# Attention with a gated spectral branch: spectral part added in the output PSUM tile, gate folded into its operand, one order of value matmuls for each kind of group, a table of keys, partial output tiles

## The chip, the cores and the metric

The kernel runs on one core of a Trainium2 chip. The metric is the device time of that core in microseconds (us), the median of several executions. Each execution also has a mean granted clock of TensorE (1.0 is full speed) and a state: "slow" when the run is over 1.5% above the fastest of the same kernel. Ratios are computed from the mean time of one kernel's fast runs over the mean time of the other's fast runs of the same rounds on the same chip, so they are not quite the ratio of the medians that are quoted. The kernel before took 421.3 us in the first measurement.

## The reference, cut to what matters

```python
def reference(A_x, A_wqkv, A_wo, B_x, B_w_r, B_w_i, gate_w):   # x: 2048 tokens x 448
    x = A_x
    g = sigmoid((x * gate_w).sum(-1, keepdims=True))           # one gate for each token
    a = full_softmax_attention(x, A_wqkv, A_wo)                # 16 heads of 28
    b = irfft2(rfft2(x) * (B_w_r + 1j * B_w_i)).astype(bf16)   # spectral mix over tokens and features
    return g * a + (1 - g) * b
```

## The kernel before

The kernel is built by a list scheduler in Python: each operation has an engine, a duration, dependences and a key (when it is due), and a simulated run fixes the order in which each engine's instructions are emitted. Each engine has its own stream of instructions in that order, with semaphores between the engines.

Attention goes over 16 groups (4 head groups x 4 chunks of 512 queries), each with 16 key tiles. TensorE makes the scores; ScalarE takes their exponentials, 3 or 2 units of 128x512 at a time, into a ring of 30 units. For some key tiles VectorE does the exponential instead: it evicts the score tile (y), and makes four shifted tiles from the integer bits (pd). TensorE multiplies ring and pd by the values (vw for the ring, vd for VectorE's tiles). The list ND says how many key tiles of each group VectorE takes, 37 in all:

```python
    ND = [0, 2, 2, 2, 2, 3, 2, 3, 2, 2, 3, 2, 3, 3, 3, 3]
```

The weights vd of VectorE's tiles are made on GpSimd, four times for each head group, each piece over three key tiles:

```python
            for f in range(4):
                def fp(f=f):
                    self.pin(nc.gpsimd.tensor_scalar(out=self.vd[:, f, :, :, 0:DH + 1], in0=self.vf[:],
                                                     scalar1=PHGAIN[f], scalar2=None, op0=ALU.mult))
```

In the background, between these, runs the spectral branch: two stages of Fourier matmuls in which a tile is evicted to one of three buffers Y and copied by DMA into a re-ordered buffer U. At its end, each output tile of 128 tokens is evicted (zt), multiplied by a last basis matrix, scaled by the complement of the gate on the way out of PSUM, and kept in SBUF (bm) until the attention part of the tile is there:

```python
            def fz(it=it, zt=zt):
                self.pin(nc.vector.tensor_copy(out=zt[0:FN].rearrange("p a b -> p (a b)"), in_=self.bgi(it)[0:FN, :]))
            # [cut: four matmuls zt x Binv into a second PSUM tile it2]
            def fb_(g=g, it2=it2):
                self.pin(nc.vector.tensor_scalar(out=self.bm[:, g, 0:D], in0=self.bgi(it2)[:, 0:D],
                                                 scalar1=self.og[:, g:g + 1], scalar2=None, op0=ALU.mult))
            # [cut]
            # output tile t, after four matmuls by wo:
            self.pin(nc.vector.scalar_tensor_tensor(out=fin[:], in0=self.bgi(it)[:, 0:D], scalar=self.gs[:, t:t + 1],
                                                    in1=self.bm[:, t, 0:D], op0=ALU.mult, op1=ALU.add))
```

All value matmuls of a group are issued in one fixed order, whether their operand comes from the ring or from VectorE: each depends on the one before (`deps = [prev_pv]`).

## Time and profile before

| | kernel before |
|---|---|
| median | 421.31 us (420.91 to 426.13) |
| span of the profiled run | 420.0 us, granted clock 0.996 |
| first exponential starts | 10.99 us |
| last exponential ends | 409.84 us |
| ScalarE busy | 403.2 us (96%) |
| VectorE busy | 349.9 us (83%) |

From the page of the kernel before: the span, the busy time of each engine, then the busy tenths of ScalarE and the granted clock in 40 slices of the span, then the share of the engines in the chain that ended last.

```profile
span 420.0 us, 12309 instructions
PE 390.9 (93%) x5207; PEld 150.9 (36%) x5207; DVE 349.9 (83%) x660; ACT 403.2 (96%) x370; POOL 30.3 (7%) x63
...
ACT  4999999999999999999999999999999999999991
...
PEclk9999999999999999999999999999899999999999
...
ACT 62%; PE 19%; issue 15%; DVE 1%; DMA 1%; ACTq 0%; DVEq 0%
```

And its costliest groups: busy time and mean length of one, then the idle time of the engine just before them and what ended most of it.

```profile
L1141 ACT ACTIVATE ring<-psA 128x1536 bf16<-128x1536 f32 x176 | 286.9, 1630 | 1.6 <-PE bg L544 0.7
L1141 ACT ACTIVATE ring<-psB 128x1024 bf16<-128x1024 f32 x175 | 212.2, 1213 | 0.0
L1099 DVE TENSOR_SCALAR y<-bg 128x512 uint16<-128x512 f32 x148 | 99.7, 684 | 14.6 <-PE bg L544 11.5
L1109 DVE TENSOR_SCALAR pd<-y 128x2048 uint16<-128x2048 uint16 x148 | 99.2, 686 | 0.6
```

ScalarE is busy from the second slice to the last but one, and its 351 exponentials are preceded by 1.6 us of idle time in all. The stream of exponentials is the bound. In these names psA and psB are the score tiles of three and of two units, bg the two PSUM banks for the background work, and pvb the bank of the value matmuls. Read in the timeline of ScalarE, the starts of two exponentials that follow each other without a stop are taken as 1.343 us apart after one of three units and 0.917 us after one of two, so 2.26 us for a pair (most lie between 1.330 and 1.347 us, and between 0.903 and 0.922 us). In the rest of this document "the stream lost" means: the time from the first to the last start of an exponential, less the sum of these two numbers over the exponentials between. The kernel before lost 2.6 us in that sense.

### The profile page before, as it was taken

What the parts mean: (1) busy time and instruction counts of PE and PEld (TensorE: products, weight loads), DVE (VectorE), ACT (ScalarE), POOL (GpSimd) and SP (SyncE); (2) the same over time, 40 slices, a digit from 0 to 9 for tenths busy, and PEclk for the clock granted to TensorE, in tenths of its full rate; (3) what the DMA queues carried; (4) which work ended last, traced back from release to release, by engine and by line L of the source; (5) the groups of instructions that cost most, each with busy time, mean ns of one, the idle gap of its engine ahead of it and who ended that gap; (6) DMA issues with size and microseconds to landing.
All of it is one profiled execution on the core that took longest, in us unless ns stands there. A gap on an engine that the chain in (4) does not pass through costs nothing.

```text
span 420.0 us, 12309 instructions
## 1 busy us (share of the span) xinstructions
PE 390.9 (93%) x5207; PEld 150.9 (36%) x5207; DVE 349.9 (83%) x660; ACT 403.2 (96%) x370; POOL 30.3 (7%) x63
## 2 busy tenths in 40 slices
PE   7899999999999989898998999899999999999996
PEld 5444333333443233233433334334343233323334
DVE  5555878878787999999989998986878999798964
ACT  4999999999999999999999999999999999999991
POOL 4302200000004000000040000000021000000000
PEclk9999999999999999999999999999899999999999
DMA  8500010001412211100110112211001110100011
GB/s 221 138 2 4 6 37 2 3 2 48 119 47 69 70 48 43 23 25 22 25 43 14 34 47 83 63 34 30 1 4 54 27 27 2 45 3 23 26 35 55
DMA packets 25915, 16.85 MB, mean 40 GB/s; under 512 B 10456, under 2 KB 24580, under 8 KB 25860
## 3 DMA queue, kind: packets, MB, share of 16 engines
q1 hardware_dynamic: 25092, 15.82, 14.3%
q8 instruction: 40, 0.66, 0.7%
q10 hardware_dynamic: 768, 0.25, 0.3%
q14 instruction: 15, 0.12, 0.1%
HBM read 10.19 MB, written 1.84 MB: 29 GB/s over the span
## 4 chain that ended last, share of the span: by engine, by line
ACT 62%; PE 19%; issue 15%; DVE 1%; DMA 1%; ACTq 0%; DVEq 0%
ACT ring L1141 61%; PE bg L544 8%; PE psA L544 4%; PE pvb L544 3%; PE psB L544 3%; DMA U<-in_A_wqkv_dram 1%; ACT w L947 0%; DVE k L888 0%; DVE q L888 0%; DVE q L735 0%; DVE k L904 0%; DVE xT L842 0%; ACT fin L1338 0%; ACT sq L718 0%; ACT q L719 0%
## 5 line engine op out<-in xcount | busy, mean ns | idle before, releaser
L1141 ACT ACTIVATE ring<-psA 128x1536 bf16<-128x1536 f32 x176 | 286.9, 1630 | 1.6 <-PE bg L544 0.7
L1141 ACT ACTIVATE ring<-psB 128x1024 bf16<-128x1024 f32 x175 | 212.2, 1213 | 0.0
L1099 DVE TENSOR_SCALAR y<-bg 128x512 uint16<-128x512 f32 x148 | 99.7, 684 | 14.6 <-PE bg L544 11.5
L544 PEld LDWEIGHTS <-k 32*128 32x128 bf16 (+1 forms) x1088 | 50.1, 91 | 140.5 <-issue 131.7
L1109 DVE TENSOR_SCALAR pd<-y 128x2048 uint16<-128x2048 uint16 x148 | 99.2, 686 | 0.6
L544 PE MATMUL psA<-q,k 32*128 32x512 bf16 x526 | 70.0, 383 | 18.1 <-ACT ring L1141 13.6
L544 PE MATMUL pvb<-ring,vw 128*32 128x512 bf16 x876 | 80.9, 387 | 0.0
L544 PE MATMUL psB<-q,k 32*128 32x512 bf16 x350 | 69.0, 382 | 2.5 <-ACT ring L1141 2.0
L544 PE MATMUL pvb<-pd,vd 128*32 128x512 bf16 x592 | 58.7, 386 | 0.0
L544 PE MATMUL bg<-q,k 32*128 32x512 bf16 x148 | 54.7, 384 | 0.3 <-DVE fin L1360 0.2
L544 PEld LDWEIGHTS <-vw 128*32 128x32 bf16 x876 | 21.6, 96 | 19.2 <-issue 15.4
L544 PEld LDWEIGHTS <-xT 128*128 128x128 bf16 (+3 forms) x512 | 19.2, 96 | 17.1 <-issue 14.5
L1434 DVE CAST Y<-bg 128x450 bf16<-128x450 f32 x32 | 19.6, 622 | 4.4 <-PE bg L544 3.1
L1008 POOL TENSOR_SCALAR vd<-vf 128x348 bf16<-128x348 f32 x16 | 17.6, 1101 | 59.9 <-DVE vf L997 43.1
L544 PE MATMUL bg<-X,R 128*32 128x225 bf16 (+1 forms) x384 | 20.7, 295 | 0.6 <-DVE y L1099 0.2
L544 PEld LDWEIGHTS <-vd 128*32 128x32 bf16 x592 | 15.4, 95 | 15.5 <-issue 13.6
L544 PE MATMUL bg<-xT,wpq 128*32 128x512 bf16 (+1 forms) x240 | 19.1, 383 | 0.0
L544 PE MATMUL bg<-xT,wpk 128*32 128x512 bf16 (+2 forms) x244 | 18.8, 382 | 0.0
L544 PE MATMUL bg<-Bd,xT 128*32 128x450 bf16 (+1 forms) x256 | 17.9, 358 | 0.3
L544 PE MATMUL bg<-Bd,ZT 113*32 113x448 bf16 x256 | 17.6, 357 | 0.3 <-DVE y L1099 0.2
L952 POOL CAST vw<-w 128x16 bf16<-128x16 f32 (+1 forms) x7 | 2.4, 349 | 192.1 <-ACT w L947 192.1
L1404 DVE CAST X<-bg 128x450 bf16<-128x450 f32 x16 | 10.0, 624 | 7.4 <-PE bg L544 7.4
(119 smaller groups left out, 340.1 us busy)
## 6 DMA issues: line engine op xcount, KB each, us to landing
U<-Y SPq DMA_DIRECT2D x32, 112.5 KB
CR<-cRB SPq DMA_DIRECT2D x8, 256.0 KB
xtok<-in_A_x_dram SPq DMA_DIRECT2D x4, 448.0 KB
out_dram<-fin SPq DMA_DIRECT2D x14, 112.0 KB
CR<-cCS SPq DMA_DIRECT2D x8, 192.0 KB
Wg<-in_B_w_r_dram SPq DMA_DIRECT2D x8, 112.5 KB
Wg<-in_B_w_i_dram SPq DMA_DIRECT2D x8, 112.5 KB
U<-in_A_wqkv_dram SPq DMA_DIRECT2D x2, 252.0 KB
```

Of the source, the lines that this page charges most:

```text
L544: self.pin(self.nc.tensor.matmul(out, lhsT=lhsT, rhs=rhs, start=start, stop=stop, **kw))
L952: self.pin(nc.gpsimd.tensor_copy(out=free_dims(self.vw[g][:], [[128, nb], [32, 4]], kt0 * 128 + DH), in_=self.w[g][:, kt0:kt0 + nb, :]))
L1008: self.pin(nc.gpsimd.tensor_scalar(out=self.vd[:, f, :, :, 0:DH + 1], in0=self.vf[:], scalar1=PHGAIN[f], scalar2=None, op0=ALU.mult))
L1099: self.pin(nc.vector.tensor_scalar(out=ys[:, s, :], in0=self.bgi(it), scalar1=127 * UNITS, scalar2=0.0, op0=ALU.add, op1=ALU.max))
L1109: self.pin(nc.vector.tensor_scalar(out=fl(pds).bitcast(U16), in0=fl(ys), scalar1=float(PHASE[f]), scalar2=0.25, op0=ALU.add, op1=ALU.mult))
L1141: self.pin(nc.scalar.activation(out=self.ring[:, u0:u0 + len(st), :], in_=slot[:, 0:len(st), :], func=ACT.Exp, scale=LN2 / UNITS))
L1404: self.pin(nc.vector.tensor_copy(out=self.X1[:, t, :], in_=self.bgi(it)[:, 0:F2]))
L1434: self.pin(nc.vector.tensor_copy(out=y[:], in_=self.bgi(it)[:, 0:F2]))
```

## The change

The intent is to give ScalarE less to do. Six more key tiles go to VectorE, and VectorE gets the room for it from the spectral branch: its result is no longer evicted on its own, but accumulated by TensorE into the same PSUM tile as the attention part of the output. As the eviction multiplies that tile by g, the spectral operand has to be multiplied by (1 - g)/g beforehand. That is a factor for each token, needed along the free dimension, the same in all partitions; so the gate, which lies one token to a partition, is written to DRAM and read back as rows. The buffer that receives the rows is the space of the transposed input xT, free by then: the profile calls the read "xT<-escr". Besides: the value matmuls keep an order only within their kind (ring, VectorE); six of the last eight output tiles are collected early in SBUF ("partial"); and a table of some 3,000 offsets to the keys, tuned on the scheduler's model, moves single operations.

```diff
-    ND = [0, 2, 2, 2, 2, 3, 2, 3, 2, 2, 3, 2, 3, 3, 3, 3]
+    ND = [1, 2, 3, 3, 2, 3, 3, 3, 2, 3, 3, 3, 3, 3, 3, 3]
@@ the schedule
+PTN, PTD = 6, 20.0
+KOFF = (
+    (0, -792), (1, -467), (2, -98), (3, 22), (4, -413), ...      [cut: the table of keys, about 3,000 entries]
+        for i, v in KOFF:
+            o = self.ops[i]
+            o.key += v / 10.0
@@ the gate
+        m = self.dve(0.09, lambda: self.pin(nc.vector.tensor_scalar(out=self.ge[:], in0=self.ge[:], scalar1=1e30,
+                                                                    scalar2=None, op0=ALU.min)), (e,), due)
+        d = self.dma(self.escr[:].rearrange("t p -> p t"), self.ge[:], (m,), due + 20.0, dur=0.5, lat=8.0)
+        src = self.escr[:]
+        self.erop = [self.dma(self.erow[b][0:FN], _AP(tensor=src.tensor, offset=src.offset + 1024 * b,
+                                                      ap=[[0, FN], [1, 1024]]), (d,), due + 30.0, dur=0.5, lat=6.0)
+                     for b in range(2)]                          # FN = 113
@@ value matmuls: one order for each kind of group
-                deps = [prev_pv]
+                deps += fd.get(kind, [])
@@ the spectral operand, with the gate folded in
-                self.pin(nc.vector.tensor_copy(out=zt[0:FN].rearrange("p a b -> p (a b)"), in_=self.bgi(it)[0:FN, :]))
+                self.pin(nc.vector.tensor_tensor(out=self.ZT[0:FN, g, :].rearrange("p (a b) -> p a b", a=4),
+                                                 in0=self.bgi(it)[0:FN, :].rearrange("p (a b) -> p a b", a=4),
+                                                 in1=free_dims(self.erow[g // 8][0:FN], [[0, 4], [1, P]], P * (g % 8)),
+                                                 op=ALU.mult))
@@ an output tile: four matmuls by wo, then the four spectral ones into the same PSUM tile
+        for j in () if part else range(4):
+            def fz(j=j):
+                self.zmm(self.bgi(it), t, j, False, j == 3)
-            self.pin(nc.vector.scalar_tensor_tensor(out=fin[:], in0=self.bgi(it)[:, 0:D], scalar=self.gs[:, t:t + 1],
-                                                    in1=self.bm[:, t, 0:D], op0=ALU.mult, op1=ALU.add))
+                self.pin(nc.vector.tensor_scalar(out=fin[:], in0=self.bgi(it)[:, 0:D], scalar1=self.gs[:, t:t + 1],
+                                                 scalar2=None, op0=ALU.mult))
[cut: the partial tiles, the two 450-wide products by the weights made one of 900, one eviction for the norms of q and k
 together, the tail, other constants of the schedule]
```

## The prediction

> **What bounds the kernel now.** ScalarE's exp stream. In the profile's timeline of ScalarE the first exp starts at 10.99 us and the last ends at 409.84 us; in between ScalarE's row of the 40 slices reads 9 throughout, and the groups view gives its 351 exps only 1.6 us of idle time. A pair of exps (3 units of 128x512 out of one score tile, 2 out of the other) starts every 2.26 us: 0.92 + 1.34 us, so 0.42 us per unit and about 0.07 us per instruction. [...]876 units at that rate are 396 of the 399 us. The rest of the span is 11.0 us of head and 10.2 us of tail. VectorE is 83% busy (349.9 us), 95% in the 160:280 us stretch; TensorE 93%, which overstates it since its records overlap.
>
> **What the change does.** By instruction counts of the two programs:
> - Key tiles whose exp is done on VectorE: 37 to 43. ScalarE's units 876 to 852, exps 351 to 341.
> - VectorE: +24 score evictions and +24 shifts, 0.60 us apart back to back (records of 0.68): +28.8 us. Removed: 16 spectral evictions with the gate (-9.6), 3 norm-row evictions (-1.8); the two 450-wide products by the weights become one of 900 (estimate 1.09 us from 0.622 us at 450[...]; about -1). Added: 6 partial-tile evictions (+3.6). The spectral product keeps about its 0.69 us though it now multiplies. Net about +20 us: 370 us, 90% of a shorter span.
> - TensorE: +18 groups of four value matmuls at 0.22 us (+4 us), 10 fewer score steps with their switches (-4), the four identity matmuls gone: even.
> - The gate in token-row form takes a round trip through DRAM, long before it is used.
> - Tail: of the last four output tiles, 13 and 15 need only one product, since their other parts are already in SBUF; 12 and 14 can collect theirs earlier. Before, 16 matmuls of 0.19 us and the transposes were mixed into 410.2 to 415.9 us.
>
> **On the critical path.** The 24 units: (876-852)/5 x 2.26 = 10.8 us, all on it while ScalarE stays saturated. The tail gives an estimated 0.8 us of its 10.2 (evictions now end at 416.9). Head unchanged. Against that: with VectorE at 90% and only two background PSUM banks, some late shifts or late slots of the exp ring (30 units, 13.6 us of slack) should stall ScalarE: I allow 1 us. The free order of value matmuls and the tuned table are there to hide just that. VectorE's and TensorE's own savings are worth nothing directly; they pay for the six key tiles.
>
> 421.3 - 10.8 - 0.8 + 1.0 = about 410.7 us. Range 406.5 to 416.5 us; faster by over 2% 0.73, within 2% 0.25, slower 0.02.
>
> **What would show it.** Exp pairs still 2.26 us apart, first exp at about 11 us, last end near 399 us; ScalarE's idle time inside the stream under 4 us; VectorE's busy time 365 to 375 us with slices at 9 from the fifth on; 172 evictions and 172 shifts of unchanged length; the 900-wide product near 1.09 us; the tail from the last exp to the end near 9.3 us.
>
> **What would make it wrong.** VectorE falling behind in the middle (waits of the value matmuls on shifted tiles, then of scores or exps on the ring), more than 4 us; a dip in the granted TensorE clock (before had one, 0.91 around 300 us) where TensorE has no slack; a gate or spectral product that arrives late; a key table tuned for durations that the chip does not have. Faster than the range only if the head shrinks too.

"That rate" of the 876 units is the measured one, 2.26 us for five, so 396 us. For the 900-wide product, the trace of the kernel before has VectorE's product vw<-bg,w at 0.382 us for 224 elements a partition and 0.619 us for 448, which is 1.06 ns for an element; 0.622 us and another 450 of these are an estimate of 1.10 us. Two other remarks of the prediction, with their numbers from the same trace: matmul records overlap (two of 0.35 us start at 412.15 and 412.34 us, 0.19 us apart), and a score step with its switches comes to 0.43 us, ten of them to 4 us (groups of value matmuls start 0.22 us apart, at 202.41 and 202.63 us; with a score step between them, 0.65 us apart, at 202.84 and 203.49 us).

## The result, and the profile after

The changed kernel took 467.38 us (median of 4 runs, 461.0 to 503.82) against 421.85 us before: ratio of the fast runs 1.1007, interval 1.0863 to 1.1151. The result is correct; the time is 10% longer where 2.5% less was predicted.

The run of 503.82 us was the profiled one. It is slow (granted clock 0.718), so its trace is not compared here. The first experiment, a1_again, is the same kernel once more; its runs are all fast (467.43 us, 465.36 to 469.18; ratio 1.1068, interval 1.101 to 1.1126), and its trace stands for the changed kernel. From its page, the same lines as of before:

```profile
span 466.4 us, 12611 instructions
PE 411.6 (88%) x5351; PEld 156.3 (34%) x5351; DVE 368.3 (79%) x678; ACT 396.2 (85%) x360; POOL 32.2 (7%) x63
...
ACT  4999999999928999999968999972434999999991
...
PEclk9999999999958999998968999866675999999999
...
PE 43%; ACT 29%; DMA 11%; issue 7%; DVE 7%; POOL 2%; ACTq 0%; DVEq 0%; POOLq 0%
...
L1499 ACT ACTIVATE ring<-psA 128x1536 bf16<-128x1536 f32 x171 | 261.4, 1529 | 17.6 <-PE psA L869 16.8
L1499 ACT ACTIVATE ring<-psB 128x1024 bf16<-128x1024 f32 x170 | 188.0, 1106 | 35.5 <-PE psB L869 19.4
L1457 DVE TENSOR_SCALAR y<-bg 128x512 uint16<-128x512 f32 x172 | 114.4, 681 | 16.6 <-PE bg L869 15.2
```

The counts are as predicted (341 exponentials, 172 evictions y), and an eviction y is as long as before (681 ns, before 684). But ScalarE's row has holes near 130 us and from 300 to 360 us, and its exponentials waited 53.1 us (17.6 + 35.5) where they had waited 1.6. The stream lost 57.5 us. The granted clock is low in the same slices: 0.50 from 320 to 330 us and again from 350 to 360 us, 0.76 and 0.75 in the two stretches of 10 us between. And DMA, 1% of the chain before, is 11% of it. The view of waits says which, in us in total, number of times, and the longest:

```profile
DVE Y L1838 <- DMA U<-Y: 25.7, 2, 13.0
PE bg L869 <- DVE Y L1838: 24.7, 3, 12.7
ACT ring L1499 <- PE psB L869: 19.4, 11, 13.3
...
PE bg L869 <- DMA r<-rhl: 8.3, 1, 8.3
```

Twice VectorE waits 13 us for a copy U<-Y, because it may not overwrite a buffer Y whose copy has not landed. In its timeline nothing else of it runs meanwhile (first time: the instruction before ends at 314.80 us, the next starts at 327.80 us); then TensorE waits for VectorE (12.7 us) and ScalarE for TensorE (13.3 us). Once TensorE waits 8.3 us for a copy r<-rhl, a reciprocal of the softmax sums on its way to another layout. Neither copy was touched by the change. What is new in the DMA queue just before each of the long waits is a gate row. The queue's timeline (start, length of the issue):

```profile
307.00 0.26 SPq L851 DMA_DIRECT2D xT<-escr  x1
310.07 2.44 SPq L851 DMA_DIRECT2D U<-Y  x1
312.56 0.45 SPq L851 DMA_DIRECT2D CR<-cRB  x1
313.12 4.58 SPq L851 DMA_DIRECT2D U<-Y  x1
...
330.16 0.24 SPq L851 DMA_DIRECT2D xT<-escr  x1
```

And the DMA engines in the 18.5 us that follow it, 307.5 to 326 us, in 40 slices: their mean busy share in tenths, then GB/s.

```profile
DMA  1000000000004686001000034100010000000000
GB/s 9 0 27 27 27 27 27 27 27 27 27 27 87 215 306 248 18 27 62 27 18 27 27 71 157 69 27 27 27 39 27 18 27 27 27 27 27 27 27 27
```

There is a floor of 27 GB/s through the whole window, while the mean busy share reads 0. In the trace the packets of the read, of 4,096 bytes, start one after the other, 0.155 us apart (in the trace of the slow run mostly 0.155 to 0.162 us). From 340 to 350 us, during the second read, the mean busy share of the 16 engines is 0.07 at 26 GB/s; one engine of 16 would be 0.06. So it is read here as the work of one of the sixteen engines. The read moves 113 rows of 4,096 bytes, 462,848 bytes, which at 27 GB/s is 17.1 us.

The 25.7 us of waits for U<-Y and the 8.3 us for r<-rhl are 34 us. The stream lost 57.5 us. What the rest is, and whether the copies really waited because of the gate, the experiments had to tell.

### The profile page after: what moved, and what is told of

The parts are those of the page before. It is cut to its first block, busy times and chain, and to the rows that moved or that the text cites. A ratio compares the mean times of both kernels' runs of the same rounds, so it can differ in the third digit from the quotient of the medians.

```text
span 502.0 us, 12611 instructions
## 1 busy us (share of the span) xinstructions
PE 456.3 (91%) x5351; PEld 157.7 (31%) x5351; DVE 375.3 (75%) x678; ACT 413.0 (82%) x360; POOL 31.6 (6%) x63
## 4 chain that ended last, share of the span: by engine, by line
PE 72%; DMA 10%; ACT 8%; DVE 4%; issue 2%; POOL 2%; ACTq 0%; POOLq 0%; DVEq 0%
PE bg L869 32%; PE pvb L869 21%; PE psA L869 10%; PE psB L869 10%; ACT ring L1499 8%; DMA U<-Y 7%; POOL vd L1363 2%; DMA r<-rhl 2%; DMA xtok<-in_A_x_dram 1%; DVE y L1457 1%; DMA U<-in_A_wqkv_dram 1%; DVE pd L1467 1%; PE bg L878 1%; DVE Y L1838 0%; DVE vw L1344 0%
## 5 line engine op out<-in xcount | busy, mean ns | idle before, releaser
L1499 ACT ACTIVATE ring<-psA 128x1536 bf16<-128x1536 f32 x171 | 248.1, 1451 | 30.4 <-PE psA L869 23.6
L1499 ACT ACTIVATE ring<-psB 128x1024 bf16<-128x1024 f32 x170 | 174.4, 1026 | 39.5 <-PE psB L869 18.9
L1457 DVE TENSOR_SCALAR y<-bg 128x512 uint16<-128x512 f32 x172 | 115.3, 685 | 26.3 <-PE bg L869 23.3
L1467 DVE TENSOR_SCALAR pd<-y 128x2048 uint16<-128x2048 uint16 x172 | 114.0, 684 | 0.5
L869 PEld LDWEIGHTS <-k 32*128 32x128 bf16 (+1 forms) x1088 | 38.8, 92 | 162.9 <-issue 160.0
L869 PE MATMUL bg<-q,k 32*128 32x512 bf16 x172 | 70.1, 435 | 13.5 <-DVE Y L1838 12.5
L869 PE MATMUL pvb<-pd,vd 128*32 128x512 bf16 x688 | 73.9, 463 | 2.3 <-POOL vd L1363 2.3
L869 PE MATMUL bg<-wvr,xT 128*128 128x112 bf16 (+1 forms) x192 | 16.4, 252 | 11.7 <-DVE Y L1838 11.7
L1363 POOL TENSOR_SCALAR vd<-vf 128x348 bf16<-128x348 f32 x16 | 18.5, 1157 | 96.4 <-PE pvb L869 69.9
L869 PE MATMUL bg<-Bd,xtok 113*32 113x448 bf16 x256 | 20.6, 418 | 0.0
L869 PE MATMUL bg<-wo,q 128*32 128x448 bf16 x248 | 20.0, 406 | 0.2 <-DVE fin L1758 0.2
## 6 DMA issues: line engine op xcount, KB each, us to landing
U<-Y SPq DMA_DIRECT2D x32, 112.5 KB
Wg<-in_B_w_i_dram SPq DMA_DIRECT2D x8, 112.5 KB
Wg<-in_B_w_r_dram SPq DMA_DIRECT2D x8, 112.5 KB
```

The costliest lines, as they stand in the source:

```text
L869: self.pin(self.nc.tensor.matmul(out, lhsT=lhsT, rhs=rhs, start=start, stop=stop, **kw))
L1457: self.pin(nc.vector.tensor_scalar(out=ys[:, s, :], in0=self.bgi(it), scalar1=127 * UNITS, scalar2=0.0, op0=ALU.add, op1=ALU.max))
L1467: self.pin(nc.vector.tensor_scalar(out=fl(pds).bitcast(U16), in0=fl(ys), scalar1=float(PHASE[f]), scalar2=0.25, op0=ALU.add, op1=ALU.mult))
L1499: self.pin(nc.scalar.activation(out=self.ring[:, u0:u0 + len(st), :], in_=slot[:, 0:len(st), :], func=ACT.Exp, scale=LN2 / UNITS))
```

## The experiments

Fourteen kernels ran, all with correct results. The first group of four ran on one chip beside 7 runs of the kernel before (median 421.10 us).

### a1_again: the changed kernel once more

No edit.

> The changed kernel once more, to get a trace of its ordinary state. All theories: 461 to 468 us. Theory 1 (one DMA engine): the profile again shows three stops of ScalarE, about 6.7, 12.4 and 13.6 us, just after the gate's write to DRAM and its two reads back (33 us in all), with DMA traffic near 26 GB/s in the last two. Theory 2 (granted TensorE clock): the clock is lower all through the kernel and exps wait for scores in all stretches, little of it in the three stops. Theory 3 (schedule too full): waits are spread over the middle at a clock near 1.0.

Measured: 467.43 us, all four runs fast; it is the profile shown above.

### a2_rows128: the gate rows read into 128 partitions

```diff
-        self.erop = [self.dma(self.erow[b][0:FN], _AP(tensor=src.tensor, offset=src.offset + 1024 * b,
-                                                      ap=[[0, FN], [1, 1024]]), (d,), due + 30.0, dur=0.5, lat=6.0)
+        self.erop = [self.dma(self.erow[b], _AP(tensor=src.tensor, offset=src.offset + 1024 * b,
+                                                ap=[[0, P], [1, 1024]]), (d,), due + 30.0, dur=0.5, lat=6.0)
```

The 15 added rows are never used, and no engine's order changes. It moves 13% more bytes.

> Only the two reads of the gate rows are made 128 instead of 113 partitions wide (same instruction order on all engines). Theory 1: [...]the copy ran on one DMA engine, 113 packets of 4096 bytes one after the other at 0.159 us (18 us); with 128 rows it takes about 2 us, both stops go, and with them the cold clock after each: 26 us plus about 4, so 430 to 438 us. Theory 2 and 3: no change, 458 us or more.

Measured: 438.63 us, ratio 1.04 (1.0347 to 1.0453), 28.8 us less than a1_again and 0.6 us above the expected range. The waits for U<-Y are no longer in the list. The DMA engines in the same window, 307.5 to 326 us, in a2:

```profile
DMA  0000000199931004594045201024287679653510
GB/s 0 0 0 0 0 0 0 62 354 363 186 133 53 0 0 80 190 378 168 0 72 175 20 0 35 0 49 138 98 319 248 239 306 392 213 171 74 156 43 14
```

The floor is gone; the read, issued at 310.09 us, is the burst of up to 363 GB/s from the eighth slice on, at a busy share of 0.9 or more in three slices. The six slices from 310.7 to 313.5 us moved 532 KB, and the read is 524 KB, so it took about 2.8 us, where about 2 had been expected. So the reads of 113 rows are shown to be the cause of the two long stops. That the copies U<-Y queued behind the read, on one engine that both need, is the reading of it and was not shown: the trace does not number the engines. What is shown is that the first wait for U<-Y ends at 327.80 us, when the floor, which lasts to about 328.4 us, is nearly over, and that there is no such wait when the read moves at up to 363 GB/s. Why 128 rows spread over the engines and 113 do not, these runs do not show.

### a3_gate_rows: the gate written in rows of 128 bytes

In the change, the write of the gate turns [128 partitions, 16] into [16, 128] by its access pattern, 2,048 elements of 4 bytes. Here VectorE transposes the 16 columns first, in blocks of 32 x 32, and four copies write 16 rows of 128 bytes each. On top of a2.

```diff
+            self.pin(nc.vector.transpose(out=self.geT[:], in_=self.ge32[:]))
-        d = self.dma(self.escr[:].rearrange("t p -> p t"), self.ge[:], (m,), due + 20.0, dur=0.5, lat=8.0)
+            for q in range(4):
+                self.pin(nc.sync.dma_start(out=self.escr[:, 32 * q:32 * q + 32], in_=self.geT[32 * q:32 * q + NT, :]))
```

> As a2, and the gate is also transposed on VectorE first, so that its write to DRAM is 64 packets of 128 bytes instead of 2048 packets of 4 bytes. Theory 1: the first stop (6.7 us, value rows waiting for the reciprocal rows' copy) goes too: 6 to 9 us below a2, 423 to 431 us. Theory 2 and 3: as a2 within 1 us.

Measured: 426.14 us, ratio 1.0072 (0.9998 to 1.0146), 12.5 us less than a2, where 6 to 9 us had been expected. (One of the four runs is slow. By the ratios of the fast runs it is 3.3% of about 421 us, 13.8 us.) The matmul that needs r, in the timeline of TensorE, in a1_again:

```profile
135.86 0.61 PE L869 MATMUL bg<-r,cst 8*32 8x512 bf16 x4 [8.30 <-DMA r<-rhl]
```

and in a3 (in brackets the idle time before it and what ended it):

```profile
133.54 0.40 PE L871 MATMUL bg<-r,cst 8*32 8x512 bf16 x4 [1.62 <-DVE pd L1478]
```

The profile puts this wait down to a pd, which the matmul does not read; the copies of r had been issued only from 130.72 to 132.0 us. The wait fell from 8.3 to 1.6 us, and the halved clock after it is gone: from 125 to 165 us the granted clock is 0.83 in a2 and 1.00 in a3. A write that nobody waits for had held up a small one that TensorE needs. The pages count its pieces: 12,552 packets under 512 bytes in a2, 10,616 in a5 below, where the same data goes in 64 rows; 1,936 fewer.

Together a2 and a3 took back 41.3 us. 15.4 us were still missing to the prediction (426.1 - 410.7).

### b1_tiles43: the kernel before, with only the new list of tiles

```diff
-    ND = [0, 2, 2, 2, 2, 3, 2, 3, 2, 2, 3, 2, 3, 3, 3, 3]
+    ND = [1, 2, 3, 3, 2, 3, 3, 3, 2, 3, 3, 3, 3, 3, 3, 3]
```

> The kernel before with only the number of VectorE key tiles raised from 37 to 43. If the six key tiles pay by themselves: 24 units of exp less, 408 to 414 us. If VectorE is what limits then (it gets 28.8 us more and none of the savings): 418 us or more, with ScalarE idle inside the exp stream for 8 us or more.

Measured: 449.98 us, ratio 1.0667 (1.0611 to 1.0723). The stream lost 32.9 us, 16.6 of them before 50 us. ScalarE waited 17.6 us, in eight times, for value matmuls to free the ring ("ACT ring <- PE pvb"). So the six tiles alone are a loss. That without the rest of the change VectorE's tiles arrive late, and that in one fixed order all later value matmuls wait behind them, is the reading of these waits; of the two, c4_bone below tests the order.

### The second group: what is left after the two DMA faults

The next four ran on another chip (before: 421.09 us). In a3 TensorE waited 1.6 us at the start for a block of x, because the table of keys had put the load of the third block before that of the second. a5_head exchanges them; a3's other suspects are undone one by one.

```diff
 # a5_head: a3 and
+            e = {1: 2, 2: 1, 3: 3}[b]
-            self.d_x.append(self.dma(self.xtok[:, 4 * b:4 * b + 4, 0:D], self.x[:, 4 * b:4 * b + 4, :], (), K + b, ...
+            self.d_x.append(self.dma(self.xtok[:, 4 * e:4 * e + 4, 0:D], self.x[:, 4 * e:4 * e + 4, :], (), K + b, ...
 # c1_b: a3 and
-PTN, PTD = 6, 20.0
-KOFF = ( ... )
+PTN, PTD = 6, 18.0
+KOFF = ()
 # c3_b37: c1_b and
-    ND = [1, 2, 3, 3, 2, 3, 3, 3, 2, 3, 3, 3, 3, 3, 3, 3]
+    ND = [0, 2, 2, 2, 2, 3, 2, 3, 2, 2, 3, 2, 3, 3, 3, 3]
 # c4_bone: c1_b and
-                deps += fd.get(kind, [])
+                deps += pvs[-1:]
```

> The kernel a3_gate_rows with one more edit: at emission the load of the second block of x comes before that of the third (the key table had exchanged them). Instruction order on the compute engines is the same as in a3. Theory (load order): in a3 TensorE waited 1.61 us for the second block at 11.4 us and the first exponential began at 12.37 us against 10.99 us before; so the wait goes, the first exponential begins at 10.5 to 11.2 us, and the time is 1.2 to 4 us under a3 (about 426 us there), 422 to 425 us. Rival (the head is lost to the low granted clock and to the density of the added tiles, and the load wait hides under it): the first exponential moves by at most 1.4 us and the time stays within 1 us of a3.

Measured: 427.28 us, ratio 1.0106 (1.0049 to 1.0162). The first exponential starts at 10.93 us instead of 12.37 us and the head's wait is gone, as the theory of the load order said; the time is not better at all. What was won at the head was lost again: by 60 us the stream had lost 2 us against 5 in a3, in the end 20.4 us against 12.4. The four runs of a5 took 422.79, 426.22, 428.33 and 430.37 us (the last is the profiled one; at 1.8% over the fastest it is counted as slow), at granted clocks of 0.983, 0.972, 0.964 and 0.960. Time and clock go together. The clock of that profiled run is not that of the slow run of the changed kernel, whose records hold 0.752, once for 129.7 us at a stretch, with stretches of 0.50 between, and never 1.0; it is 1.00 with stretches of 0.50, as in the fast runs of a3 and a6, so it is used below for where the stretches lie, and a6 and a7, both fast, for what they cost.

> The kernel a3_gate_rows without the table of keys (every key is what the rules give; the lead of the first partial tiles is 18 instead of 20 us, because with 20 the kernel's own order check refuses it). Theory (the table is what makes 43 key tiles on VectorE fit): without it the stream loses what the 43 tiles alone lost in b1 (32.9 us), so 440 to 455 us. Rival (the table is worth a few us, and the freed VectorE work is what makes the tiles fit): 424 to 434 us.

Measured: 428.90 us, ratio 1.0162 (1.0122 to 1.0203). The rival held, for this state of the kernel: without the table the time is about that of a5.

> The kernel c1_b with the old list of 37 key tiles on VectorE instead of 43. The ideal stream is longer by 10.8 us. Theory (43 tiles are over what this order can feed without the table): it is faster than c1_b, and lies within 2% of the kernel before, 416 to 429 us. Rival (43 tiles fit by themselves): it is 6 to 11 us slower than c1_b.

Measured: 425.80 us, ratio 1.0107 (1.0073 to 1.0141). The stream lost 4.8 us, against 14.8 in c1_b. It is a shade faster than c1_b, but the two intervals touch, so the order of the two stays undecided. What is plain is that the shorter stream of 43 tiles gained nothing here.

> The kernel c1_b in which the value matmuls are issued in one fixed order across kinds of group (each waits for the one before it), as in the kernel before, instead of each kind with its own order. Theory (the freedom of order matters little, as it moves matmuls by less than the pipeline's slack): within 1% of c1_b. Rival (the order is a part of what the change gains): slower than c1_b by over 4 us.

Measured: 431.03 us, ratio 1.0229 (1.0208 to 1.025). The total is within 1% of c1_b, but that hides a difference: the stream lost 14.2 us before 48 us (c1_b: 4.3 us), with one wait of 10.2 us of ScalarE for a value matmul, where the longest of c1_b is 1.8 us. It is the wait that b1 had. The free order removes it.

### The third group: short waits of TensorE

In a5's trace the clock was halved at four places: from 129.4 us for 6.8 us, from 207.9 us for 3.4 us, from 228.4 us for 13.7 us and from 293.3 us for 10.2 us. Before the first and the third stands a wait of TensorE of only 1 to 2 us; before the other two there is none over 0.6 us. The first wait is again at the matmul that reads r (the profile names a pd, as in a3; in a8_vd_only below it names r<-rhl). In the queue's timeline of a5:

```profile
120.67 0.61 SPq L853 DMA_DIRECT2D rs<-pvs  x1
124.25 1.73 SPq L1387 DMA_DIRECT2D escr<-geT  x4
126.08 1.27 SPq L853 DMA_DIRECT2D r<-rhl  x2
```

The four writes of the gate that a3 had made out of one stand in the queue just before the copies of r, which were ready at 124.9 us. The other wait is for vd. TensorE's timeline of a5:

```profile
226.06 0.40 PE L871 MATMUL pvb<-pd,vd 128*32 128x512 bf16 x4 [0.69 <-POOL vd L1369]
226.39 0.39 PE L871 MATMUL psB<-q,k 32*128 32x512 bf16 x2
226.71 0.40 PE L871 MATMUL bg<-r,cst 8*32 8x512 bf16 x4
228.36 0.61 PE L871 MATMUL pvb<-pd,vd 128*32 128x512 bf16 x4 [1.26 <-POOL vd L1369]
228.90 0.61 PE L871 MATMUL psA<-q,k 32*128 32x512 bf16 x3
```

A score matmul takes 0.39 us before the waits and 0.61 us after them. a6_write issues the gate's writes later; a7_vd makes vd in smaller pieces, the key tile that is used first in all four phases before the rest.

```diff
 # a6_write: a5 and
         def wr():
-            for q in range(4):
-                self.pin(nc.sync.dma_start(out=self.escr[:, 32 * q:32 * q + 32], ...
+            self.later = [20, wr_now]      # the same four writes, behind the next 20 DMAs of this queue
 # a7_vd: a6 and
                 def fp(f=f):
-                    self.pin(nc.gpsimd.tensor_scalar(out=self.vd[:, f, :, :, 0:DH + 1], in0=self.vf[:],
-                                                     scalar1=PHGAIN[f], scalar2=None, op0=ALU.mult))
+                    todo = ([(p, 2, 3) for p in range(4)], [(0, 0, 2), (1, 0, 2)], [(2, 0, 2), (3, 0, 2)], [])[f]
+                    for p, a, z in todo:
+                        self.pin(nc.gpsimd.tensor_scalar(out=self.vd[:, p, a:z, :, 0:DH + 1], in0=self.vf[:, a:z],
+                                                         scalar1=PHGAIN[p], scalar2=None, op0=ALU.mult))
```

> The kernel a5_head with one more edit: the four small writes of the gate to DRAM, which the DMA queue issued from 124.25 to 125.98 us, between the request for a row of sums and the two copies of their reciprocals (r<-rhl, ready at 124.9 us, issued at 126.08 us), are issued 27 us later, where nothing is waiting in that queue. All else keeps its order. Theory (a wait of TensorE of 1 to 2 us is followed by several us of a halved granted clock, and that is what the stream still loses): the wait of 1.6 to 2.0 us at 128.9 us shrinks below 0.8 us, the granted clock stays at 1.0 from 128 to 140 us[...], the stream loses under 4 us by 160 us instead of 6.1 us, and the time is 2 to 5 us under a5 (about 427), 422 to 425 us. Rival (the low clock comes from the amount of work on TensorE and not from the wait): the clock drops there all the same, and the time is within 1 us of a5.

Measured: 424.93 us, ratio 1.0049 (0.9989 to 1.0109). From 124 to 142 us the granted clock is 1.00 where a5 had 0.81, the longest wait of TensorE there is 0.3 us, and the stream had lost 3.1 us at the 120th exponential instead of 6.1. The median is 2.4 us under a5, at the near end of the expected 2 to 5; the intervals of a5 and a6 overlap. The wait and the clock did what was expected, but the saving in the total is not resolved by these runs, and the clock there is not decided by the wait alone: in a3 a wait of 1.62 us at the same matmul left it at 1.00, where in a5 one of 1.61 us was followed by 6.8 us at half.

> The kernel a6_write with one more edit: the scaled values of the VectorE tiles (vd), which GpSimd made in four pieces of 1.08 to 1.36 us, one for each phase and each over three key tiles, are made key tile 15 first, in eight smaller pieces, so that what is used first is there 2 to 3 us earlier. Theory as for a6: TensorE's two waits for vd at 226 and 228 us (0.69 and 1.26 us) go, the clock stays at 1.0 from 226 to 254 us, where it was 0.76, the 7.3 us that the stream lost there in a5 go to under 2 us, and the time is 3 to 7 us under a6: 416 to 421 us, level with or under the kernel before. Rival: the waits go, the clock is as low as before, and the time is within 1.5 us of a6.

Measured: 412.79 us, ratio 0.979 (0.9764 to 0.9817), all runs between 412.65 and 414.35 us, 12.1 us under a6. a6 and a7 are one edit apart. Around the wait for vd, which in a6 ends at 223.86 us after 1.26 us: busy time and number of instructions of TensorE, its weight loads, VectorE, ScalarE and GpSimd, then the granted clock, the DMA share and GB/s, in stretches of the trace (us from the start), a6 first:

```profile
225.00:229.00 4.00, 3.80 (x34) 0.91 (x30) 2.99 (x6) 3.40 (x3) 0.00 (x0) 0.62 0.00 0
229.00:233.00 4.00, 4.00 (x30) 0.67 (x27) 2.42 (x4) 2.48 (x2) 0.00 (x0) 0.50 0.00 0
233.00:237.00 4.00, 4.00 (x44) 1.07 (x41) 3.32 (x5) 2.64 (x3) 0.00 (x0) 0.60 0.00 0
```

and a7:

```profile
225.00:229.00 4.00, 3.88 (x56) 1.26 (x52) 4.00 (x8) 4.00 (x4) 0.00 (x0) 1.00 0.00 0
229.00:233.00 4.00, 4.00 (x67) 1.43 (x65) 4.00 (x10) 4.00 (x5) 0.00 (x0) 1.00 0.40 107
233.00:237.00 4.00, 3.40 (x56) 1.30 (x48) 4.00 (x7) 4.00 (x4) 0.00 (x0) 1.00 0.03 6
```

In a6 TensorE is busy nearly all the time and yet issues 108 matmuls in these 12 us (34 + 30 + 44), where a7 issues 179; ScalarE is fed for 8.52 us of the 12. The wait was 1.26 us; the half clock behind it held for 10.2 us. The expectation had been 416 to 421 us; it came out better, because the third low stretch (290 to 306 us, mean clock 0.68 in a5 and 0.76 in a6) went as well, to 1.00. The page of a7, lines as before:

```profile
span 410.9 us, 12631 instructions
PE 389.7 (95%) x5351; PEld 153.4 (37%) x5351; DVE 366.7 (89%) x679; ACT 392.7 (96%) x360; POOL 40.3 (10%) x80
...
ACT  4999999999999999999999999999999999999981
...
PEclk9999999999999999999999999999999999999999
...
L1521 ACT ACTIVATE ring<-psA 128x1536 bf16<-128x1536 f32 x171 | 267.7, 1565 | 0.7 <-PE psA L876 0.6
L1521 ACT ACTIVATE ring<-psB 128x1024 bf16<-128x1024 f32 x170 | 194.8, 1146 | 0.9 <-PE pvb L876 0.9
```

The stream of a7 runs from 10.83 to 398.87 us and lost 2.7 us, as in the kernel before. This is the version that beats both kernels; by 2.1% over the kernel before, and whether the true figure is a little under 2% the interval leaves open.

The trace keeps the granted clock as stretches with a start, a length and a value. All stretches of 0.50 inside the spans of these kernels are whole numbers of 3.413 us (one in the kernel before, three in the 10.2 us of a6). In the 12 us above TensorE issued 108 matmuls for 179 at a mean clock of 0.57, so an estimate of what such stretches cost is half of their sum, as long as TensorE has no slack. Beside what the stream lost, in us (the profiled run of each):

| kernel | time at clock 0.50 | half of it | the stream lost |
|---|---|---|---|
| before | 3.4 | 1.7 | 2.6 |
| a3_gate_rows | 17.1 | 8.5 | 12.4 |
| a5_head | 34.1 | 17.1 | 20.4 |
| a6_write | 23.9 | 11.9 | 14.8 |
| a7_vd | 0 | 0 | 2.7 |
| a8_vd_only (below) | 23.9 | 11.9 | 12.4 |

Two of these profiled runs (a5, a8) are counted as slow, and for these stretches alone; the others are fast. The halves account for nearly all that these kernels lose beyond the 2.7 us of a7. The waits themselves are a small part. All of the changed kernels in this table have the table of keys. For the kernels without it the same estimate falls short: 5.1 of 14.8 us in c1_b, 5.1 of 22.4 us in c4_bone, 1.7 of 4.8 us in c3_b37.

### The fourth group: controls

```diff
 # d1_before_vd: the kernel before, with only the edit of vd of a7
 # d2_nokeys:    c1_b (no table of keys) with the edits of a6 and a7
 # a8_vd_only:   a3 with only the edit of vd of a7
 # a9_rows113:   a7 and
-        self.erop = [self.dma(self.erow[b], _AP( ... ap=[[0, P], [1, 1024]]), ...
+        self.erop = [self.dma(self.erow[b][0:FN], _AP( ... ap=[[0, FN], [1, 1024]]), ...
```

> Control: the kernel before, with only the edit of a7 (vd made in eight pieces, key tile 15 first). The kernel before never waits long for vd and its stream loses 2.6 us in all. Theory (the gain of a7 is the change's own, which the waits had eaten): within 1 us of the kernel before. Rival (the earlier vd is a gain by itself, in any kernel): over 3 us faster than the kernel before.

Measured: 422.41 us, ratio 0.9997 (0.9951 to 1.0044). The earlier vd is worth nothing in the kernel before. So a7's gain over it belongs to the change.

> The kernel c1_b (no table of keys) with the two edits of a6 and a7: the gate's writes issued later, vd in eight pieces. Theory (the table of keys is a needed part: without it 43 tiles on VectorE cannot be fed at full pace, whatever the waits): the stream still loses 8 to 14 us, 421 to 428 us. Rival (the table is worth little, and only the waits stood in the way): 412 to 417 us, level with a7.

Measured: 429.57 us, ratio 1.0152 (1.0089 to 1.0214), a little above the expected range; the stream lost 18.5 us. The rival, which had held for c1_b, falls here: d2 and a7 differ by the table alone, with the exchanged load that belongs to it and the lead of 18 instead of 20 us for the first partial tiles, and take 429.57 and 412.79 us. But the two edits did not bring the full clock here: d2 spent 27.3 us at 0.50, estimated at 13.7 of its 18.5 us. Before the stretch from 200 us on, TensorE's only waits were of 0.67 and 0.49 us, and for ScalarE. So part of the difference is the clock. Whether it is the table that keeps it up, and how, was not found, and how short a wait is harmless cannot be said from these runs: in c4_bone a wait of 1.08 us for r<-rhl, from 137.0 us on, left the clock at 1.00.

> The kernel a3_gate_rows with only the edit of a7 (vd in eight pieces, key tile 15 first): the load order of x and the place of the gate's writes stay as the change had them. Theory (each wait costs its own length and the slow clock after it): the losses at 226 us and after 290 us go, those of the head (1.4 us later start, some 3 us by 60 us) and of the wait at 129 to 134 us (1 to 4 us) stay: 415 to 420 us. Rival 1 (the late vd was the whole of it): 412 to 414 us, level with a7. Rival 2 (one wait after another is needed, the edits only work together): 423 to 427 us, as a3.

Measured: 422.34 us, ratio 0.9954 (0.9869 to 1.004); its fast runs took 417.67 to 422.70 us, and the profiled one is slow. It lies above the range of the theory and between the two rivals. In its trace the waits for vd are gone and the clock from 220 to 254 us is 1.00, but the two other waits are there (1.3 us for x at the start, 1.6 us for r at 131 us), the clock is 0.83 from 10 to 30 us and 0.93 from 126 to 150 us, and, against the expectation, still 0.78 from 290 to 306 us. So vd is not the whole: about 4 us of the 13.4 us between a3 and a7 (medians; 5.0 of 11.9 us by the ratios of the fast runs) are had by vd alone, and the intervals of a3 and a8 overlap. The rest came only with the other two edits; the three do not add up one by one. Why the stretch from 290 us is slow in a5, a6 and a8 and not in a3 and a7 is not settled: no wait of TensorE over 0.6 us stands before it.

> The kernel a7_vd with only the two gate-row reads put back to 113 partitions, as the change has them (one DMA engine instead of sixteen). Theory (two stops of everything, 10 to 12 us each, and slow clock after them): 434 to 446 us, so 21 to 33 us over a7, as much as a2 gained over the changed kernel (28.8 us). Rival (the stops were long only because the kernel was already behind): under 425 us.

Measured: 446.29 us, ratio 1.0551 (1.0482 to 1.0621), 33.5 us over a7, just above the expectation. The two waits of VectorE for U<-Y are back:

```profile
DVE Y L1860 <- DMA U<-Y: 25.6, 2, 13.0
```

In a kernel where no other wait is long, the number 113 in one access pattern costs about 28 us (an estimate, 33.5 less the 5.2 us that follow). Not all of the 33.5 us is the read's: in the profiled run a stretch of half clock of 10.2 us began at 280.7 us, before the first read was issued at 287.36 us, and by 296 us, where TensorE's first long wait begins, the stream had lost 7.8 us against 2.6 us in a7. This is the stretch near 290 us again. Up to it TensorE's waits were no longer than in a7 (from 215 us on at most 0.61 us in both), and yet the clock was halved here and not there. So the waits for vd cannot be all that decides about that stretch, and the part of a7's gain over a6 that comes from it is not explained.

## Why the prediction was wrong

Point by point:

- **The bound.** Right. ScalarE's stream bounds the kernel before, and a7 again: last exponential at 398.87 us, predicted "near 399 us". A unit takes 0.426 us in the trace (1.343 - 0.917).
- **The gain of the six tiles.** Right in its mechanism and size. The stream took 398.85 us before (10.99 to 409.84) and 388.04 us in a7 (10.83 to 398.87): 10.8 us less, as predicted. In the changed kernel as it stands, it is more than eaten up.
- **VectorE's load.** Right: 368.3 us busy in a1_again and 366.7 in a7 (predicted 370, band 365 to 375), 172 evictions of 0.68 us, and the 900-wide product took 1.083 us (predicted 1.09).
- **"The gate in token-row form takes a round trip through DRAM, long before it is used."** This is the step that failed. The prediction asked only whether the gate would be late, and it never was. It did not ask what the round trip does to other copies that are in flight. Costed at nothing, it cost 28.8 us for the reads of 113 rows (a2 against a1_again; 33.5 us in a9 against a7), and 12.5 us for the write in 4-byte pieces (a3 against a2), both with the halved clock that followed. Of 56.7 us between the predicted 410.7 and the measured 467.4 us, these are 41.3.
- **"I allow 1 us" for stalls.** Too little, though the kind of trouble was named ("a dip in the granted TensorE clock ... where TensorE has no slack"; "a key table tuned for durations that the chip does not have"). The remaining waits are small: x loaded out of order by the table, the place of the gate's write, and vd, which the scheduler's model counts as 0.6 us a piece and the chip ran in 1.21 us (mean of 16 in a1_again). The edits that removed them took 13.4 us off (a3 426.14, a7 412.79); by the traces most of that is time at half clock, and for one such stretch, near 290 us, no wait was found that explains it.
- **The free order and the table.** "There to hide just that": right. Without the order the start of the stream stopped for 10.2 us (c4; the total rose by only 0.7% by the ratios), and without the table 43 tiles were not fed at pace even with the long waits gone (d2, 429.57 us).
- **The tail.** Predicted 9.3 us from the last exponential to the end; in a7 it is 12.0 us (410.9 - 398.87), before 10.2 us. In a7's timeline 12 matmuls by wo and 16 spectral ones run only from 405.87 us on, with only four more matmuls by wo behind them. The reading is that with two background PSUM banks, collecting tiles "earlier" had no bank to do it in. The 2.7 us of the tail are enough for the 2.1 us between 412.8 and the predicted 410.7; their cause was read from the timeline and not tested.

With these faults mended, then, the change does what was predicted, within 2.1 us. The prediction was of the change as written.

## What to carry to other kernels

When a change adds a DMA that is needed only much later, cost it by what else is in flight: look in a trace at what its shape lets it move (here 27 GB/s for 113 partitions against a burst of up to 363 for 128), how small its pieces are, and what stands behind it in its queue. Here reads that nobody waited for stood before two waits of up to 13.0 us for copies of 112.5 KB, and a write in 2,048 pieces of 4 bytes before a wait of 8.3 us for one of 4 KB. In a kernel whose TensorE and ScalarE are near 95% busy, look in the trace for waits of TensorE of even 1 us and at the granted clock behind them; a wait of 1.26 us, beginning 1.05 us after one of 0.52 us, was followed by 10.2 us of halved clock (a6), and the clock stayed at 1.00 when they were gone (a7). It is a thing to test and not a rule: a wait of 1.62 us was followed by none (a3), and some halved stretches had no such wait before them (a5 from 207.9 us, a9 from 280.7 us). And when a tuned version is slower than the old one, mend the waits one at a time before judging the idea: the edits did not add up singly (by medians 1 us lost, then 2 and 12 us won, in the order in which they were made), and the last one brought the kernel from level to 2% ahead.
